# A delta-rule attention feeding two expert layers: the host transposes Q, and a block of Q is scaled by one number and split in place

## The chip, the cores and the metric

One core of a Trainium2 chip runs the whole program. The metric is device time in microseconds (us) of one execution, lower is better. Engines are named as in the profile: PE (matrix multiplies), PEld (its weight loads), DVE (vector), ACT (scalar/activation), POOL (GpSimd), SP (the queue that issues most transfers).

## The reference, cut to what matters

```
def _attn_ref(q, k, v, beta):                 # B=4, H=8, S=768, D=48
    k_n = k / (norm(k, axis=-1) + 1e-6)
    state = zeros((B, H, D, D))
    for t in range(S):
        y[:, :, t] = einsum('bhd,bhde->bhe', q[:, :, t], state)
        v_old = einsum('bhde,bhd->bhe', state, k_n[:, :, t])
        state = state + beta_t * einsum('bhd,bhe->bhde', k_n[:, :, t], v[:, :, t] - v_old)
    return y
# x = y as (3072, 384)
# x = moe(x):  8 experts, all of them on every row, weights from a Sinkhorn iteration on x @ w_gate
# out = moe2(x): 8 experts, one for each row (argmax), relu(x @ w1[e]) @ w2[e]
```

## The kernel before

Attention is cut into 12 chunks of 64 tokens; a chunk of two of the four batches is one **block**, so there are 24 blocks, `block(i)`. In a tile of a block, 128 partitions hold two batches by 64 tokens, or two batches by 64 places of which 48 are features, and the free axis holds the 8 heads. Numbers that need more than half precision are carried as two float16 tiles, a high part and a low part ("split"), and multiplied as three products.

For each block the **front** loads K, Q (one tile `KQ`, one transfer of `kq[c, pr]`) and V, takes sums of squares (`sqk`, `sqq`, `sqv` on ACT, the first ones reduced by `ssr` on DVE), normalises K (`rc1` to `rc5`, `kn`) and gets power-of-two scales (`scl`). K is split by `kh`, `kl`. Q has a scale for each of its rows: `qs` scales it, `qh` and `ql` split it into `KQ1[:, 2:4]`. K and Q each then go the same way: `kpd`/`qpd` put the two halves of the partitions into a block-diagonal tile (`KPB`, `QTB`) by two transfers on SP (for the first three blocks by copies on DVE and ACT), `kt0`, `kt1`/`qt0`, `qt1` (line 643) transpose on PE against an identity, 8 multiplies of 64 columns each, and `ke0`, `ke1`/`qe0`, `qe1` (lines 506 and 508, `kqc<-pz`) move the result from PSUM to the compact tile `KQc`, which has three buffers and has K in columns 0 to 63 of each head and Q in 64 to 127. From there `kb` and `qtd` make the block-diagonal `KTB` and `QTB` by further transfers, and `gp0`, `gp1` (line 660) multiply K by both. The rest of the block is a doubling recursion of five levels (`z`, `Z`, `a`, `t`, `tt`), the update of the state and the output (`y0`, `y1`, last score multiply `pl`, `lgs` on line 819).

At the same time `moe_unit` runs the first two experts on finished blocks: first-layer multiplies on line 849 (256 columns), second layer on 873 (384 columns), with ACT on 860 and 883 and DVE on 862. There are 2160 of these multiplies in 24 units. This overlapped stage is called the **weave** below. When its last unit is done, PE goes on with line 1085 and then with the other experts.

The order of all instructions of the weave on each engine is fixed when the program is built, by the class `Sched`: a list scheduler with a cost in ns for each operation, a priority (the block number less an advance) and free choice of engine where a node names several, as `(("A", 413), ("V", 270))`. So a changed cost or a changed node reorders the rest. Names of a node's engines: P is PE, A ACT, V DVE, G POOL, D the SP queue.

The next load into `KQ` waits for the last reader of the block before, since `KQ` has one buffer:

```
N("ld", "D", 1300, f, [("kl", pb), ("ql", pb), ("kn", pb), P4("r2l"), P4("sqv")] ...)
```

Of the kernel before, what the change touches and what calls it, by code (L numbers as in the profile page):

```python
# [19 lines left out]
C = 64  # L20
# [146 lines left out]
def kernel(  # L167
# [274 lines left out]
    with (  # L442
# [74 lines left out]
        def block(i):  # L517
# [21 lines left out]
            def front(name, shape, dt, at):  # L539
                if i == 1:  # L540
                    o[name] = hhl[:, at:at + (1 if dt is F16 else 2) * shape[0] * shape[1] * (shape[2] if len(shape) > 2 else 1)]
                    o[name] = o[name].bitcast(dt)
                    if len(shape) == 3:
                        o[name] = o[name].rearrange("p (a b c) -> p a b c", a=shape[0], b=shape[1])
                    else:
                        o[name] = o[name].rearrange("p (a b) -> p a b", a=shape[0])
                    return o[name]
                return tl(name, shape, dt, 0)
# [26 lines left out]
            def f():  # L575
                front("KQ1", [4, 8, 48], F16, 1536)
                tl("ss", [10], F32, par)
                nc.scalar.activation(out=o["KQ1"][:, 2], in_=o["Q"], func=AF.Square, accum_out=o["ss"][:, 8:9])
            N("sqq", "A", 510, f, ["ld", ("kpd", pb), ("qpd", pb), ("rc2", i - 2), ("par", i - 2)])
            N("sqv", "A", 510, lambda: nc.scalar.activation(  # L580
                out=o["KQ1"][:, 3], in_=o["V"], func=AF.Square, accum_out=o["ss"][:, 9:10]), ["sqq"])
# [4 lines left out]
            N("sq", "A", 220, lambda: nc.scalar.activation(out=tl("sr", [10], F32, par)[:, 0:9], in_=o["ss"][:, 0:9], func=AF.Sqrt),  # L586
              ["ssc", ("pq", i - 2), ("rc3", i - 2)])


            def f(slot):  # L590
                o["sv"] = pcp.tile([128, 1], F32, name="sv", tag=f"pc{slot}")
                nc.tensor.matmul(out=o["sv"], lhsT=ones32, rhs=o["ss"][:, 9:10], start=True, stop=True)
            N("sv", "P", 250, f, ["ssc"], ps=("pc", 1))
            N("par", "A", 200, lambda: nc.scalar.activation(out=o["sr"][:, 9:10], in_=o["sv"], func=AF.Sqrt), ["sv", "sq"], frees="sv")
            N("rc1", "V", 120, lambda: nc.vector.reciprocal(out=tl("rc", [8], F32, par), in_=o["sr"][:, 0:8]), ["sq", ("kn", i - 2)])
# [5 lines left out]
            N("kn", (("V", 470), ("G", 790)), 0, lambda e: ttt(e, o["K"], o["K"], o["rc"].unsqueeze(2).to_broadcast([128, 8, 48]), ALU.mult), ["rc5"])  # L601
            N("kh", (("A", 413), ("V", 270)), 0, lambda e: cpy(e, o["KQ1"][:, 0], o["K"]), ["kn"])
            N("kl", VG4, 0, lambda e: ttt(e, o["KQ1"][:, 1], o["K"], o["KQ1"][:, 0], ALU.subtract), ["kh"])

            BD("kpd", lambda: KPB[nb], lambda: o["KQ1"][:, 0:2], ["kl", P4("ds"), ("zK", nb)])

# [9 lines left out]
            else:  # L616
                NN[("pm", i)] = NN[("pq", i)]
            N("px_", "V", 70, lambda: nc.vector.tensor_scalar(
                out=o["scl"][:, 2:4].bitcast(U32), in0=o["scl"][:, 0:2].bitcast(U32), scalar1=EXPMASK, scalar2=None, op0=ALU.bitwise_xor), ["pm"])
            N("qs", "A", 507, lambda: nc.scalar.activation(out=o["Q"], in_=o["Q"], func=AF.Copy, scale=o["scl"][:, 2:3]), ["px_", "sqq"])  # L620
            N("vs", "A", 507, lambda: nc.scalar.activation(out=o["V"], in_=o["V"], func=AF.Copy, scale=o["scl"][:, 3:4]), ["px_", "sqv"])
            N("qh", (("A", 413), ("V", 270)), 0, lambda e: cpy(e, o["KQ1"][:, 2], o["Q"]), ["qs"])
            N("p3", "V", 75, lambda: nc.vector.tensor_tensor(
                out=o["scl"][:, 5:6], in0=o["scl"][:, 1:2], in1=c3[:, 1:2], op=ALU.mult), ["pm", ("cs", 0)])
            N("p4", "V", 70, lambda: stt(o["scl"][:, 7:8], o["scl"][:, 0:1], 0.125, o["scl"][:, 1:2], ALU.mult), ["pm"])
            N("ql", VG4, 0, lambda e: ttt(e, o["KQ1"][:, 3], o["Q"], o["KQ1"][:, 2], ALU.subtract), ["qh", "sqv"])

            BD("qpd", lambda: QTB[nb], lambda: o["KQ1"][:, 2:4], ["ql", P4("y1"), P4("qtd"), ("zQ", nb)])

# [5 lines left out]
            N("mb", (("V", 602), ("G", 1001)), 0, f, [("ml", i - NPS), ("m16", i - NPS), ("tt0", i - NPS), "kn", ("cs", 0), ("bt2", 0)])  # L635
            for x, nm, dep in ((0, "k", "kpd"), (1, "q", "qpd")):
                src = KPB[nb] if x == 0 else QTB[nb]
                for y in range(2):
                    def f(slot, x=x, y=y, src=src):
                        o["KQc"] = KQC[sl]  # L640
                        t = o[f"t{x}{y}"] = pzt(slot)
                        for h in range(H):
                            nc.tensor.matmul(out=t[:, h], lhsT=src[:, y, h], rhs=I16, start=True, stop=True)
                    N(f"{nm}t{y}", "P", 235, f, [dep, ("gp1", i - NPS), ("qtd", i - NPS), ("cs", 0)], ps=("pz", 1), cols=512)
                    N(f"{nm}e{y}", AV5, 0, lambda e, x=x, y=y: cpy(e, o["KQc"][:, y, :, 64 * x:64 * x + 64], o[f"t{x}{y}"]),
                      [f"{nm}t{y}"], frees=f"{nm}t{y}")
            BD("kb", lambda: KTB[nb], lambda: o["KQc"][:, :, :, 0:64], ["ke0", "ke1", P4("ks"), P4("gp1"), ("zT", nb)])

            def f():
                for b2 in range(2):  # L650
                    bd_half(QTB[nb], o["KQc"][:, :, :, 64:128], b2, nc.sync.dma_start)
            N("qtd", "D", 1300, f, ["qe0", "qe1"])
            for u in range(2):
                hs = slice(4 * u, 4 * u + 4)

                def f(slot, u=u):
                    pg = o[f"pg{u}"] = pzp.tile([128, 4, 128], F32, name="pg", tag=f"pz{slot}")
                    for h in range(4 * u, 4 * u + 4):
# [167 lines left out]
        def moe_unit(e, r):  # L826
# [14 lines left out]
            for g4 in range(nf // per):  # L841
                for j in range(per):
                    f_ = per * g4 + j
                    for kk in range(KD):
# [940 lines left out]
```

## Time and profile before

| | |
|---|---|
| median of 3 runs | 2178.95 us (2176.89 to 2179.65) |
| the profiled execution's own time | 2180.95 us |
| its span, first to last instruction | 2179.2 us |
| mean granted PE clock | 0.98 of full |
| busy: PE, DVE, ACT, POOL | 2052.1, 1230.6, 851.4, 261.5 us |

Busy times are shares of the whole span. The weave is its first 675 us; what an engine does there is read from that stretch alone. [...]

### The profile page before, as it was taken

What the parts mean: (1) busy time and instruction counts of PE and PEld (TensorE: products, weight loads), DVE (VectorE), ACT (ScalarE), POOL (GpSimd) and SP (SyncE); (2) the same over time, 40 slices, a digit from 0 to 9 for tenths busy, and PEclk for the clock granted to TensorE, in tenths of its full rate; (3) what the DMA queues carried; (4) which work ended last, traced back from release to release, by engine and by line L of the source; (5) the groups of instructions that cost most, each with busy time, mean ns of one, the idle gap of its engine ahead of it and who ended that gap; (6) DMA issues with size and microseconds to landing.
All of it is one profiled execution on the core that took longest, in us unless ns stands there. A gap on an engine that the chain in (4) does not pass through costs nothing. (4 is left out here: it accounts for less than half of the span.)

```text
span 2179.2 us, 46134 instructions
## 1 busy us (share of the span) xinstructions
PE 2052.1 (94%) x19340; PEld 1298.1 (60%) x19340; DVE 1230.6 (56%) x2828; ACT 851.4 (39%) x1598; POOL 261.5 (12%) x304
## 2 busy tenths in 40 slices
PE   4689999999998889999999999999999999999999
PEld 3567777777764435555555555555555555557776
DVE  7989888888771564555555455555552245552111
ACT  7766666666531332222222222222231134453332
POOL 3233232322200000000000000000000000113221
PEclk9699999999999989999999999999999999999999
DMA  7456655566534233113203113212300001058765
GB/s 255 91 110 116 120 108 111 114 122 129 124 90 167 95 99 116 55 62 116 88 30 116 59 58 117 87 44 102 116 30 1 1 15 30 19 174 331 257 236 205
DMA packets 372006, 235.14 MB, mean 108 GB/s; under 512 B 302588, under 2 KB 349600, under 8 KB 365394
## 3 DMA queue, kind: packets, MB, share of 16 engines
q1 hardware_dynamic: 366354, 220.32, 35.2%
q0 software_dynamic: 4288, 10.25, 1.4%
q8 instruction: 154, 2.52, 0.5%
q10 hardware_dynamic: 1152, 1.57, 0.2%
q14 instruction: 58, 0.48, 0.1%
HBM read 146.94 MB, written 51.93 MB: 91 GB/s over the span
## 5 line engine op out<-in xcount | busy, mean ns | idle before, releaser
L355 PE MATMUL pt<-big,W 128*128 128x512 f16 x2304 | 508.9, 381 | 9.3 <-DVE hhl L339 5.3
L355 PEld LDWEIGHTS <-W 128*128 128x128 f16 x2304 | 226.3, 98 | 281.4 <-issue 16.4
L366 PE MATMUL py<-W,hhl 128*128 128x384 f16 x1632 | 287.1, 327 | 3.5 <-DVE accb L385 3.4
L366 PE MATMUL py<-W,ttb 128*128 128x384 f16 x1440 | 253.6, 326 | 0.0
L338 ACT ACTIVATE hhl<-pt 128x512 f16<-128x512 f32 x136 | 81.1, 597 | 415.5 <-PE pt L355 415.3
L366 PEld LDWEIGHTS <-hhl 128*128 128x128 f16 x1632 | 160.1, 98 | 114.4 <-issue 6.0
L366 PEld LDWEIGHTS <-ttb 128*128 128x128 f16 x1440 | 140.9, 98 | 93.1
L385 DVE SCALAR_TENSOR_TENSOR accb<-py,pet,accb 128x384 f32<-128x384 f32 x136 | 83.8, 616 | 185.8 <-PE py L366 184.2
L849 PE MATMUL pt<-xring,W 128*128 128x256 f16 x1296 | 181.3, 278 | 2.2 <-ACT xring L506 1.0
L339 DVE SCALAR_TENSOR_TENSOR hhl<-pt,hhl 128x512 f16<-128x512 f32 x136 | 93.9, 690 | 153.1 <-ACT hhl L338 153.1
L873 PE MATMUL py<-W,hhl 128*128 128x384 f16 x864 | 175.3, 330 | 4.0 <-ACT yo L883 3.1
L339 DVE SCALAR_TENSOR_TENSOR ttb<-pt,ttb 128x512 f16<-128x512 f32 x120 | 83.0, 691 | 108.4 <-ACT ttb L338 108.4
L338 ACT ACTIVATE ttb<-pt 128x512 f16<-128x512 f32 x120 | 71.6, 597 | 151.4 <-PE pt L355 151.4
L298 DVE TENSOR_REDUCE wmx<-st 128x1 f32<-128x512 f32 x168 | 109.8, 676 | 33.2 <-DMA st<-in_moe_w_dram 33.2
L849 PEld LDWEIGHTS <-W 128*128 128x128 f16 x1296 | 115.4, 100 | 17.2 <-issue 1.8
L305 POOL PARTITION_ALL_REDUCE wma<-wm x28 | 10.1, 362 | 949.8 <-DVE wm L303 949.8
L1299 PEld LDWEIGHTS <-W 128*128 128x128 f16 x1008 | 90.7, 98 | 50.8 <-issue 0.3
L1319 PE MATMUL py<-W,hhl 128*128 128x384 f16 x624 | 108.9, 326 | 0.0
L1305 DVE SCALAR_TENSOR_TENSOR ttb<-pt,ttb 128x512 f16<-128x512 f32 x50 | 34.6, 692 | 117.7 <-ACT ttb L1304 117.7
L873 PEld LDWEIGHTS <-hhl 128*128 128x128 f16 x864 | 74.2, 100 | 41.5 <-issue 6.7
L1299 PE MATMUL pt<-big,W 128*128 128x512 f16 x432 | 97.7, 379 | 0.0
L1305 DVE SCALAR_TENSOR_TENSOR hhl<-pt,hhl 128x512 f16<-128x512 f32 x52 | 35.8, 688 | 87.2 <-ACT hhl L1304 87.1
(367 smaller groups left out, 3173.6 us busy)
## 6 DMA issues: line engine op xcount, KB each, us to landing
st<-in_moe_w_dram SPq DMA_DIRECT2D x28, 1536.0 KB, 9.5
W<-w2d SPq DMA_DIRECT2D x18, 1536.0 KB, 8.4
w2d<-big SPq DMA_DIRECT2D x16, 1536.0 KB, 6.2
big<-w2d SPq DMA_DIRECT2D x8, 1536.0 KB, 6.5
accb<-w2d SPq DMA_DIRECT2D x8, 1536.0 KB, 8.6
big<-kqc SPq DMA_DIRECT2D x90, 128.0 KB, 3.4
KQ<-in_kq_dram SPq DMA_DIRECT2D x23, 384.0 KB, 3.6
big<-KQ SPq DMA_DIRECT2D x84, 96.0 KB, 3.0
```

Of the source, the lines that this page charges most:

```text
L298: nc.vector.tensor_reduce(out=mx[:, c:c + 1], in_=st[:, c * CW:c * CW + CW], op=ALU.max, axis=AX.X, apply_absolute_value=True)
L305: nc.gpsimd.partition_all_reduce(ma, m1, channels=128, reduce_op=bass.bass_isa.ReduceOp.max)
L338: nc.scalar.activation(out=oh, in_=pt, func=AF.Relu)
L339: nc.vector.scalar_tensor_tensor(out=ol, in0=pt, scalar=0.0, in1=oh, op0=ALU.max, op1=ALU.subtract)
L355: nc.tensor.matmul(out=po, lhsT=lhsT, rhs=rhs, start=(i == 0), stop=(i == 3 * KD - 1))
L366: nc.tensor.matmul(out=py[:, 0:DM], lhsT=lhsT, rhs=rhs, start=(n == 0), stop=(n == 3 * (KF - fs) - 1))
L385: nc.vector.scalar_tensor_tensor(out=acc[t], in0=py[:, 0:DM], scalar=pe[x][:, t:t + 1], in1=acc[t], op0=ALU.mult, op1=ALU.add)
L849: nc.tensor.matmul(out=o[g4][:, 256 * j:256 * j + 256], lhsT=w1v(W, wv, kk, f_), rhs=XR[:, xv, kk], start=(kk == 0 and x == 0), stop=(kk = ...
L873: nc.tensor.matmul(out=o["py"][:, 0:DM], lhsT=a_[f_ // per][:, c_:c_ + 128], rhs=w2v(W, b_, f_), start=(f_ == 0 and x == 0), stop=(f_ == n ...
L1299: nc.tensor.matmul(out=po, lhsT=w1v(W, wv, kk, f), rhs=xv[:, kk, :], start=(kk == 0 and x == 0), stop=(kk == KD - 1 and x == 2))
L1305: V((f"rs{q_}", id_), lambda q_=q_: nc.vector.scalar_tensor_tensor(out=HL[q_], in0=o[q_], scalar=0.0, in1=HH[q_], op0=ALU.max, op1=ALU.sub ...
L1319: nc.tensor.matmul(out=o["py"][:, 0:DM], lhsT=a_[f // per][:, c_:c_ + 128], rhs=w2v(W, b_, f), start=(f == 0 and x == 0), stop=(f == KF - ...
```

## The change

The host writes Q as (feature, head, token) with 48 features padded to 64 places by zeros, so a row of `kq` grows from 768 to 896 numbers and Q comes in already transposed. `qh` on ACT multiplies Q by a scale and writes the high part straight into `KQc`; `ql` on DVE takes Q times the scale less that high part into the low half. `qs`, `qpd`, `qt0`, `qt1`, `qe0` and `qe1` are gone. Since rows of the new Q tile are features, the scale is one for the block: `sqq` squares 512 numbers in a row with 1/16 of each, and the multiply by ones that summed V's squares over partitions (`sv`) now sums a second column for Q.

```
 def f():
-    t = front("KQ", [2, 8, 48], F32, 0)
-    o["K"], o["Q"] = t[:, 0], t[:, 1]
-    nc.sync.dma_start(out=t.rearrange("p a h d -> p (a h d)"), in_=kq[c, pr])
+    t = front("KQ", [896], F32, 0)
+    o["K"], o["Q"] = t[:, 0:DM].rearrange("p (h d) -> p h d", h=8), t[:, DM:896].rearrange("p (h s) -> p h s", h=8)
+    nc.sync.dma_start(out=t, in_=kq[c, pr])
...
-    nc.scalar.activation(out=o["KQ1"][:, 2], in_=o["Q"], func=AF.Square, accum_out=o["ss"][:, 8:9])
-N("sqq", "A", 510, f, ["ld", ("kpd", pb), ("qpd", pb), ("rc2", i - 2), ("par", i - 2)])
+    nc.scalar.activation(
+        out=o["jk"][:, 0:512].rearrange("p (h s) -> p h s", h=8), in_=o["Q"], func=AF.Square, scale=1.0 / 16, accum_out=o["ss"][:, 8:9])
+N("sqq", "A", 620, f, ["ld", ("kpd", pb), ("rc2", i - 2), ("par", i - 2)])
...
-N("qs", "A", 507, lambda: nc.scalar.activation(out=o["Q"], in_=o["Q"], func=AF.Copy, scale=o["scl"][:, 2:3]), ["px_", "sqq"])
-N("qh", (("A", 413), ("V", 270)), 0, lambda e: cpy(e, o["KQ1"][:, 2], o["Q"]), ["qs"])
+o["KQc"] = KQC[sl]
+N("qh", "A", 620, lambda: nc.scalar.activation(
+    out=o["KQc"][:, 0, :, 64:128], in_=o["Q"], func=AF.Copy, scale=o["scl"][:, 2:3]), ["px_", "sqq", ("gp1", i - NPS), ("qtd", i - NPS)])
...
-N("ql", VG4, 0, lambda e: ttt(e, o["KQ1"][:, 3], o["Q"], o["KQ1"][:, 2], ALU.subtract), ["qh", "sqv"])
-
-BD("qpd", lambda: QTB[nb], lambda: o["KQ1"][:, 2:4], ["ql", P4("y1"), P4("qtd"), ("zQ", nb)])
+N("ql", "V", 602, lambda: stt(o["KQc"][:, 1, :, 64:128], o["Q"], o["scl"][:, 2:3], o["KQc"][:, 0, :, 64:128], ALU.subtract), ["qh"])
...
-N("qtd", "D", 1300, f, ["qe0", "qe1"])
+N("qtd", "D", 1300, f, ["ql", P4("y1"), P4("qtd"), ("zQ", nb)])
...
-N(f"gp{u}", "P", 680, f, ["kb", "qe0", "qe1"], ps=("pz", 2), cols=1536)
+N(f"gp{u}", "P", 680, f, ["kb", "ql"], ps=("pz", 2), cols=1536)
```

Line numbers behind the change move by two or three (643 becomes 641, 660 becomes 657, 849 becomes 846, 860 becomes 857, 873 becomes 870, 883 becomes 880, 1085 becomes 1082).

On ACT, in the front of a block in the middle of the weave, before: `qs` (620), the float16 copy of Q, V's scale (621) and evictions of transposes (`kqc<-pz`).

```order
L620 ACTIVATE KQ<-KQ,scl 128x384
L506 CAST KQ_5894<-KQ 128x384
L621 ACTIVATE V<-V,scl 128x384
L506 CAST kqc<-pz 128x8x64 x2
L883 COPY yo<-py 128x384
L506 CAST t_6148<-pz 128x512
L506 CAST tt<-pz 128x512
```

And at the same place of a block now:

```order
L620 ACTIVATE V<-V,scl 128x384
L506 CAST Et<-pz 128x512
L624 ACTIVATE kqc<-KQ,scl 128x8x64
L857 ACTIVATE hhl<-pt 128x512
L506 CAST R_6431<-V 128x384
L506 CAST t_6438<-pz 128x512
L506 CAST kqc<-pz 128x8x64 x2
```

Two passes over Q became one that writes `KQc` (line 624), and of four evictions for a block two are left. Over the whole weave ACT has 46 of them now and had 87; on DVE 2 are left of 9.

On DVE, in the same part of a block, before: the copy and the subtraction that split Q (both write `KQ_5894`, the tile `KQ1` of that block), between rows of the recursion and of `gp0`.

```order
L508 CAST KQ_5894<-KQ 128x384
L502 TENSOR_TENSOR Z<-pz,cs 128x512
L502 TENSOR_TENSOR KQ_5894<-KQ,KQ_5894 128x384
L690 STREAM_TRANSPOSE tt<-t_6148 128x512
L502 TENSOR_TENSOR W_99<-pg,W_99 128x256
L502 TENSOR_TENSOR PT<-pg,cs 128x256
```

And now, with the new subtraction `kqc<-KQ,scl,kqc`:

```order
L502 TENSOR_TENSOR Z<-pz,cs 128x512
L859 SCALAR_TENSOR_TENSOR hhl<-pt,hhl 128x512
L502 TENSOR_TENSOR W_99<-pg,W_99 128x256
L499 SCALAR_TENSOR_TENSOR kqc<-KQ,scl,kqc 128x8x64
L502 TENSOR_TENSOR PT<-pg,cs 128x256
L687 STREAM_TRANSPOSE tt<-t_5780 128x512
```

All 24 subtractions for Q stand on DVE now. In the whole weave DVE has 8 copies that split K or Q where it had 16, 15 such subtractions where it had 26, and 10 subtractions of the identity (`pi`, `W<-W,cs`) where it had 20: the other ten stand on POOL.

On ACT at the end of the attention, from the last block's copy into `xring` on, before:

```order
L506 COPY xring<-px 128x6x128
L860 ACTIVATE hhl<-pt 128x512
L984 ACT_TABLE_LOAD
L984 ACTIVATE P_103<-P_103 128x24x8
L956 ACTIVATE W_99<-st,w1s 128x512 x3
L883 COPY yo<-py 128x384 x2
L860 ACTIVATE hhl<-pt 128x512 x2
L883 COPY yo<-py 128x384 x2
L860 ACTIVATE hhl<-pt 128x512 x4
```

And now:

```order
L506 COPY xring<-px 128x6x128
L857 ACTIVATE hhl<-pt 128x512 x2
L981 ACT_TABLE_LOAD
L981 ACTIVATE P_103<-P_103 128x24x8
L880 COPY yo<-py 128x384
L953 ACTIVATE W_99<-st,w1s 128x512 x3
L880 COPY yo<-py 128x384
L857 ACTIVATE hhl<-pt 128x512 x4
L880 COPY yo<-py 128x384 x2
```

Behind the last block stand 16 hidden-layer passes (860, now 857) where 11 stood, so more of the expert units' work lies behind the attention. On PE the last score multiply stands behind 1692 of the 2160 expert multiplies; it stood behind 1812. Of the 120 that moved behind it 96 are of the first layer (849) and 24 of the second (873).

## Rows read from the trace of the kernel before

**Rows 1.** The page's head, and PE's granted clock in 40 slices of the span.
```profile
span 2179.2 us, 46134 instructions
...
PEclk9699999999999989999999999999999999999999
```

**Rows 2.** Windows: stretch, length, busy time and count of each engine, clock, DMA share.
```profile
20.00:60.00 40.00, 19.67 (x307) 17.39 (x308) 38.55 (x109) 30.96 (x63) 16.04 (x15) 0.99 0.73 205
60.00:100.00 40.00, 26.57 (x525) 23.52 (x525) 38.66 (x93) 29.54 (x56) 10.22 (x10) 0.63 0.35 69
100.00:600.00 500.00, 462.82 (x8843) 373.90 (x8840) 423.13 (x995) 311.18 (x664) 136.89 (x126) 0.97 0.59 118
600.00:675.00 75.00, 69.05 (x635) 49.69 (x631) 44.95 (x131) 23.54 (x41) 2.25 (x7) 0.98 0.26 79
```

**Rows 3.** Groups of instructions to 660 us: busy us, mean ns, idle before.
```profile
L506 ACT CAST kqc<-pz 128x512 f16<-128x512 f32 x87 | 48.7, 585 | 9.4 <-PE pz L643 8.9
...
L643 PE MATMUL pz<-c,big 128*128 128x64 f16 x768 | 38.2, 202 | 14.7 <-ACT kqc L506 4.4 <-DVE Z L502 4.4 <-ACT big L506 4.3
...
L502 POOL TENSOR_TENSOR KQ<-KQ,KQ 128x384 f16<-128x384 f32 x21 | 20.3, 969 | 25.2 <-ACT KQ L506 13.7 <-DVE KQ L508 9.4 <-ACT V L621 1.8
...
L502 DVE TENSOR_TENSOR KQ<-KQ,KQ 128x384 f16<-128x384 f32 x25 | 16.8, 674 | 1.9 <-ACT KQ L506 1.6
...
L506 ACT CAST KQ<-KQ 128x384 f16<-128x384 f32 x31 | 15.7, 505 | 4.4 <-POOL KQ L502 3.8 <-DVE KQ L502 0.4
...
L620 ACT ACTIVATE KQ<-KQ,scl 128x384 f32<-128x384 f32 x23 | 14.2, 617 | 19.8 <-DVE scl L618 19.5
...
L572 ACT ACTIVATE K<-KQ 128x384 f32<-128x384 f32 x23 | 12.1, 524 | 23.6 <-DMA KQ<-in_kq_dram 22.7 <-DVE ss L582 0.7
...
L578 ACT ACTIVATE KQ<-KQ 128x384 f16<-128x384 f32 x23 | 11.8, 513 | 3.0 <-DMA KQ<-in_kq_dram 3.0
...
L508 DVE CAST KQ<-KQ 128x384 f16<-128x384 f32 x15 | 8.6, 572 | 1.2 <-ACT KQ L620 1.2
...
L508 DVE CAST kqc<-pz 128x512 f16<-128x512 f32 x9 | 6.1, 680 | 0.0
```

**Rows 4.** Two adjacent rows of PE's timeline: start, length, line, count.
```profile
558.08 0.63 PE L643 MATMUL pz<-c,big 128*128 128x64 f16 x16
558.55 0.65 PE L873 MATMUL py<-W,hhl 128*128 128x384 f16 x3
```

**Rows 5.** The same view of groups: nearest kin of the new instructions, and `pi`.
```profile
L502 DVE TENSOR_TENSOR W<-W,cs 128x512 f32<-128x512 f32 x20 | 14.2, 712 | 0.0
...
L958 DVE SCALAR_TENSOR_TENSOR W<-xring,w0s,W 128x512 f16<-128x512 f32 x9 | 7.8, 873 | 1.1 <-ACT W L956 1.1
...
L956 ACT ACTIVATE W<-xring,w0s 128x512 f16<-128x512 f32 x9 | 6.0, 715 | 0.0
...
L502 POOL TENSOR_TENSOR W<-W,cs 128x512 f32<-128x512 f32 x4 | 5.1, 1271 | 13.3 <-DVE W L502 13.3
...
L958 DVE SCALAR_TENSOR_TENSOR W<-st,w1s,W 128x512 f16<-128x512 f32 x3 | 2.2, 739 | 0.0
```

**Rows 6.** Timeline of the weave's end: last block's result, expert multiplies, next stage.
```profile
617.31 0.23 DVE L819 TENSOR_SCALAR lg<-pl,scl 128x8 f32<-128x8 f32 x1
...
653.11 4.06 PE L873 MATMUL py<-W,hhl 128*128 128x384 f16 x24 [0.61 <-ACT yo L883]
...
657.00 4.09 PE L849 MATMUL pt<-xring,W 128*128 128x256 f16 x36
...
660.93 2.40 PE L873 MATMUL py<-W,hhl 128*128 128x384 f16 x12
...
674.78 7.93 PE L1085 MATMUL pt<-big,W 128*128 128x512 f16 x36
```

**Rows 7.** Transfers to 675 us: count, KB of each, median us from issue to landing.
```profile
KQ<-in_kq_dram SPq DMA_DIRECT2D x23, 384.0 KB, 3.6
big<-KQ SPq DMA_DIRECT2D x84, 96.0 KB, 3.0
```

More of the change, by code (lines that the diff above doesn't have):

```diff
@@ L540, in front @@
                 if i == 1:
-                    o[name] = hhl[:, at:at + (1 if dt is F16 else 2) * shape[0] * shape[1] * (shape[2] if len(shape) > 2 else 1)]
-                    o[name] = o[name].bitcast(dt)
+                    n_ = shape[0] * (shape[1] * shape[2] if len(shape) > 1 else 1)
+                    o[name] = hhl[:, at:at + (1 if dt is F16 else 2) * n_].bitcast(dt)
                     if len(shape) == 3:
                         o[name] = o[name].rearrange("p (a b c) -> p a b c", a=shape[0], b=shape[1])
-                    else:
-                        o[name] = o[name].rearrange("p (a b) -> p a b", a=shape[0])
                     return o[name]
@@ L575, in f @@
             def f():
-                front("KQ1", [4, 8, 48], F16, 1536)
+                front("K1", [2, 8, 48], F16, 1792)
                 tl("ss", [10], F32, par)
-                nc.scalar.activation(out=o["KQ1"][:, 2], in_=o["Q"], func=AF.Square, accum_out=o["ss"][:, 8:9])
-            N("sqq", "A", 510, f, ["ld", ("kpd", pb), ("qpd", pb), ("rc2", i - 2), ("par", i - 2)])
+                o["jk"] = o["K1"].rearrange("p a h d -> p (a h d)")
+                nc.scalar.activation(
+                    out=o["jk"][:, 0:512].rearrange("p (h s) -> p h s", h=8), in_=o["Q"], func=AF.Square, scale=1.0 / 16, accum_out=o["ss"][:, 8:9])
+            N("sqq", "A", 620, f, ["ld", ("kpd", pb), ("rc2", i - 2), ("par", i - 2)])
             N("sqv", "A", 510, lambda: nc.scalar.activation(
-                out=o["KQ1"][:, 3], in_=o["V"], func=AF.Square, accum_out=o["ss"][:, 9:10]), ["sqq"])
+                out=o["jk"][:, 0:DM].rearrange("p (h d) -> p h d", h=8), in_=o["V"], func=AF.Square, accum_out=o["ss"][:, 9:10]), ["sqq"])
             N("ssr", "V", 480, lambda: nc.vector.tensor_reduce(
@@ L585, in block @@
                 out=o["ss"], in0=o["ss"], scalar1=2.0 ** -18, scalar2=1e-30, op0=ALU.mult, op1=ALU.max), ["ssr", "sqv"])
-            N("sq", "A", 220, lambda: nc.scalar.activation(out=tl("sr", [10], F32, par)[:, 0:9], in_=o["ss"][:, 0:9], func=AF.Sqrt),
+            N("sq", "A", 220, lambda: nc.scalar.activation(out=tl("sr", [10], F32, par)[:, 0:8], in_=o["ss"][:, 0:8], func=AF.Sqrt),
               ["ssc", ("pq", i - 2), ("rc3", i - 2)])
             def f(slot):
-                o["sv"] = pcp.tile([128, 1], F32, name="sv", tag=f"pc{slot}")
-                nc.tensor.matmul(out=o["sv"], lhsT=ones32, rhs=o["ss"][:, 9:10], start=True, stop=True)
+                o["sv"] = pcp.tile([128, 2], F32, name="sv", tag=f"pc{slot}")
+                nc.tensor.matmul(out=o["sv"], lhsT=ones32, rhs=o["ss"][:, 8:10], start=True, stop=True)
             N("sv", "P", 250, f, ["ssc"], ps=("pc", 1))
-            N("par", "A", 200, lambda: nc.scalar.activation(out=o["sr"][:, 9:10], in_=o["sv"], func=AF.Sqrt), ["sv", "sq"], frees="sv")
+            N("par", "A", 200, lambda: nc.scalar.activation(out=o["sr"][:, 8:10], in_=o["sv"], func=AF.Sqrt), ["sv", "sq"], frees="sv")
             N("rc1", "V", 120, lambda: nc.vector.reciprocal(out=tl("rc", [8], F32, par), in_=o["sr"][:, 0:8]), ["sq", ("kn", i - 2)])
@@ L601, in block @@
             N("kn", (("V", 470), ("G", 790)), 0, lambda e: ttt(e, o["K"], o["K"], o["rc"].unsqueeze(2).to_broadcast([128, 8, 48]), ALU.mult), ["rc5"])
-            N("kh", (("A", 413), ("V", 270)), 0, lambda e: cpy(e, o["KQ1"][:, 0], o["K"]), ["kn"])
-            N("kl", VG4, 0, lambda e: ttt(e, o["KQ1"][:, 1], o["K"], o["KQ1"][:, 0], ALU.subtract), ["kh"])
-            BD("kpd", lambda: KPB[nb], lambda: o["KQ1"][:, 0:2], ["kl", P4("ds"), ("zK", nb)])
+            N("kh", (("A", 413), ("V", 270)), 0, lambda e: cpy(e, o["K1"][:, 0], o["K"]), ["kn"])
+            N("kl", VG4, 0, lambda e: ttt(e, o["K1"][:, 1], o["K"], o["K1"][:, 0], ALU.subtract), ["kh"])
+            BD("kpd", lambda: KPB[nb], lambda: o["K1"], ["kl", P4("ds"), ("zK", nb)])
             def f():
@@ L635, in block, with f @@
             N("mb", (("V", 602), ("G", 1001)), 0, f, [("ml", i - NPS), ("m16", i - NPS), ("tt0", i - NPS), "kn", ("cs", 0), ("bt2", 0)])
[L636 to L646, printed above, removed]
+            for y in range(2):
+                def f(slot, y=y):
+                    t = o[f"t{y}"] = pzt(slot)
+                    for h in range(H):
+                        nc.tensor.matmul(out=t[:, h], lhsT=KPB[nb][:, y, h], rhs=I16, start=True, stop=True)
+                N(f"kt{y}", "P", 235, f, ["kpd", ("gp1", i - NPS), ("qtd", i - NPS), ("cs", 0)], ps=("pz", 1), cols=512)
+                N(f"ke{y}", AV5, 0, lambda e, y=y: cpy(e, o["KQc"][:, y, :, 0:64], o[f"t{y}"]), [f"kt{y}"], frees=f"kt{y}")
             BD("kb", lambda: KTB[nb], lambda: o["KQc"][:, :, :, 0:64], ["ke0", "ke1", P4("ks"), P4("gp1"), ("zT", nb)])
@@ L856, in moe_unit @@
                             dep.append(("mlast", last))
-                            dep += [("kpd", 1), ("qpd", 1), ("kn", 1), ("qs", 1)]
+                            dep += [("kpd", 1), ("kn", 1), ("qh", 1), ("ql", 1)]
                         N(nm, "P", 327, f, dep, ps=("pt", 1) if j == 0 and kk == 0 else None, cols=768, moe=True)
@@ L1764, in add @@
         args.append(nc.dram_tensor(f"in_{name}_dram", a.shape, _mybir.dt.from_np(a.dtype), kind="ExternalInput").ap())
-    q_, k_, v_ = (_np.reshape(inputs[n], (2, 2, H, NC, C, D)).transpose(3, 0, 1, 4, 2, 5).reshape(NC, 2, 128, H * D) for n in "qkv")
-    inputs["kq"] = _np.concatenate([k_, q_], -1)
+    k_, v_ = (_np.reshape(inputs[n], (2, 2, H, NC, C, D)).transpose(3, 0, 1, 4, 2, 5).reshape(NC, 2, 128, H * D) for n in "kv")
+    qt_ = _np.zeros((NC, 2, 2, C, H, C), _np.float32)
+    qt_[:, :, :, 0:D] = _np.reshape(inputs["q"], (2, 2, H, NC, C, D)).transpose(3, 0, 1, 5, 2, 4)
+    inputs["kq"] = _np.concatenate([k_, qt_.reshape(NC, 2, 128, H * C)], -1)
     inputs["v"] = v_
```

## The prediction

> **What bounds the kernel now.** I read the page's head and slices first: the span is 2179.2 us and PE's clock is full nearly throughout, with one dip in the second slice [rows 1]. The windows cut the span where its nature changes [rows 2]. From 20 to 100 us DVE is busy 77.2 of 80 us while PE is about half busy: DVE sets the pace of the ramp. From 100 to 600 us PE is busy 463 of 500 us (93%), DVE 423 (85%), ACT 311 (62%), POOL 137 (27%). So in the long part of the weave PE is nearest to full and DVE second. From 600 to 675 us PE is busy 69 of 75. The timeline of the end shows the border: the last block's result comes at 617.3, then PE works off what is left of the expert units, and the next stage's first multiply starts at 674.8 [rows 6]. From there to the end of the span are 2179.2 - 674.8 = 1504.4 us whose code and order the change leaves alone. So the change can only move the point 674.8, by what it does to PE's work or to PE's waits.
>
> **PE.** Gone are `qt0` and `qt1`: 24 blocks x 2 x 8 = 384 of the 768 multiplies on line 643 (with their weight loads). The mean record of 202 ns [rows 3] is not their price, since records overlap. Sixteen of them start at 558.08 and the next line starts at 558.55 [rows 4], so 0.47/16 = 29.4 ns each, and 384 x 29.4 ns = **11.3 us**. This is at the full clock; in the ramp some run at half of it, but there PE is not what is waited for.
>
> [...]
>
> **ACT.** Gone: 24 `qs` at 617 ns and 41 evictions at 585 ns, 14.8 + 24.0 us; copies that split K or Q fall from 32 to 15, 17 x 505 ns = 8.6 us [rows 3]. New: 24 `qh` over 512 numbers with a scale read per partition, nearest kin line 956 at 715 ns [rows 5], +17.2 us; and `sqq` over 512 numbers where 384 took 513 ns [rows 3], by the step from 617 to 715 ns for the same growth +0.1 us x 24 = +2.4. Net about -28 us on an engine 62% busy: no gain by itself, but fewer late evictions.
>
> **DVE.** Gone of Q's and K's splitting: 8 copies (16 to 8) x 572 ns, 11 subtractions (26 to 15) x 674 ns, 7 evictions x 680 ns: 4.6 + 7.4 + 4.8 = 16.8 us [rows 3]. New: 24 `ql` in one pass over 512 numbers; kin line 958 took 739 ns undisturbed and 873 ns beside the weight loading of the ramp [rows 5], so 17.7 to 21.0 us. I take 17.7, since the ramp holds only the first few of 24 blocks. So the Q work on DVE comes out even (+0.9, at worst +4.2). It had been shared with POOL, which loses 13 of its 21 subtractions. What DVE does gain is that ten `pi` move to POOL: -10 x 712 ns = -7.1 us, against +10 x 1271 ns on POOL, which stood idle three quarters of the time [rows 2, 5]. Net about -6 us, bounds -7 to -3.
>
> **SP and transfers.** 42 of the 84 transfers of 96 KB from `KQ1` go, and each load grows from 384 to 448 KB [rows 7]. That removes 4.0 MB and adds 1.5 MB. DMA is 59% busy in the weave [rows 2]; I put the gain at nothing (bounds 0 and -2 us), because the waits ahead of line 643 name ACT and DVE [rows 3]. Q's path to `gp0` loses a transfer of 3.0 us, the transposes and the evictions, but K still goes that way, so `gp0` comes no sooner on that account.
>
> **Where the work goes.** The built order moves 120 expert multiplies behind the last block. From the end of the weave, 24 of the second layer take 657.00 - 653.11 = 3.89 us (162 ns) and 36 of the first 660.93 - 657.00 = 3.93 us (109 ns) [rows 6], so these 120 are 96 x 0.109 + 24 x 0.162 = 14.4 us. If PE sets the pace, the attention ends 11.3 + 14.4 = 25.7 us sooner, near 592, and the tail grows from 57.5 to 71.9 us: a gain of 11.3 at the end. If DVE sets it, the gain is its 6 us, and what PE saves turns into PE idle time. PE at 93% is nearer to full than DVE at 85%, so I stay near PE's end but not on it: **-9 us** (bounds -5 and -14). Against the profiled execution's own 2180.95 us that is 2172; this execution lay 2.0 us above the median 2178.95, so the median becomes **2170**.
>
> A difference of 0.2%, 4.4 us, is about what a measurement of this kernel can tell from none.
>
> **Rivals.**
> *More goes than the work.* Line 643 waited 14.7 us in all for evictions and PSUM buffers, and the evictions 8.9 us for it [rows 3]; half of these transposes and 48 of 96 evictions are gone. If Q's half of the waits goes (7.4 us) and ACT's relief removes a few more, the gain is 16 to 25 us: 2154 to 2163. For it: the three PSUM buffers `pz` are asked for 48 times less. Against it: PE follows a fixed order, and a wait removed at one row is often met again at the next.
>
> *DVE takes it all.* `ql` can no longer be given to POOL, and behind it on DVE stand the recursion's `Z` and `tt`, for which PE waits. If 24 x 873 ns is the price and the ten `pi` on POOL (1271 for 712 ns, ahead of `tt0` and `m16`) hand their extra 0.56 us on, the gain is 6 - 3.2 - 5.6 = -2.8, so within 4 us of none: 2175 to 2182. For it: DVE at 97% in the ramp. Against: 15% of its time free after that.
>
> *Slower: the load waits.* `KQ` has one buffer, and `ql` now cannot run before a buffer of `KQc` is free, so the next block's load starts when `ql` is done and takes 3.6 us to land [rows 7]. ACT already waits 22.7 us for these loads [rows 3], and in the new order fewer instructions stand on ACT between `qh` and the next block's first square. ACT is in order: behind that square wait the evictions for PE. If each of 23 loads costs PE 1 us more, the time is 2170 + 23 = 2193; it is slower from 13.4/23 = 0.6 us a block on. Against it: the same load waited for `ql` before too, behind `qs` and `qh`, and ACT is idle 38% of the time.
>
> [...]
>
> **How the numbers follow.** Forecast (5 to 14 us less): 0.53. More than the work: 0.18. DVE takes it: 0.17. The load waits: 0.08. The clock: 0.04. Faster by over 0.2%: the first two, less a little at the forecast's edge, 0.70; within 0.2%: 0.18, the third and that edge; slower: the last two, 0.12. The range 2158 to 2181 holds the forecast, the third case but for its edge and half of the second; what lies outside is about 0.2. The forecast's own range is 2165 to 2174.
>
> **What would show it.** In the profile after: 384 multiplies on line 641; `qh` at 0.70 to 0.73 us on ACT and `ql` at 0.72 to 0.88 us on DVE; the last `lg` between 590 and 605 us and the first multiply of line 1082 between 660 and 670; from there to the end 1504 us within 3. PE's busy time from 100 to 600 stays at 93% or above. I am wrong in the size if PE's busy share falls while DVE's rises above 90%; wrong in the sign if ACT's wait for `KQ<-in_kq_dram` grows to 45 us or more and PE's idle time grows with it, or if the clock stays near 0.6 behind 100 us. If the attention ends early but line 1082 starts at 675, the tail has eaten the gain.

## The result, and the profile after

The change made the kernel slower: 2192.6 us median (2186.5 to 2197.8, 7 runs) against 2178.8 us for the kernel before on the same chip, a ratio of 1.0057, 95% interval [1.0046, 1.0069]. (Ratios are given as they stand on record; the quotient of two medians, here 1.0063, differs from them by up to 0.1%.) I had forecast 2170 and a range of 2158 to 2181. The profiled execution after has a span of 2191.2 us.

The page's head and clock after, to be read against [rows 1]:

```profile
span 2191.2 us, 45238 instructions
...
PEclk9999999999999999999999999999999999999999
```

The windows after, with the columns of [rows 2]:

```profile
20.00:60.00 40.00, 17.32 (x238) 14.85 (x239) 31.50 (x89) 27.61 (x57) 11.59 (x11) 1.00 0.66 217
60.00:100.00 40.00, 22.14 (x400) 19.93 (x400) 38.99 (x91) 22.86 (x44) 12.37 (x11) 1.00 0.43 82
100.00:600.00 500.00, 451.36 (x8593) 361.73 (x8593) 417.33 (x992) 303.10 (x631) 142.58 (x129) 0.96 0.54 113
600.00:675.00 75.00, 70.83 (x620) 51.34 (x619) 44.13 (x124) 23.31 (x40) 2.26 (x7) 1.00 0.21 66
```

From 100 to 600 us PE is busy 11.5 us less than before, DVE 5.8 and ACT 8.1 less. All three engines do less, and all three stand idle longer; PE's share is 90%, where the prediction wanted 93% or above. Part of this is work that now stands behind 600 us. Over the whole weave, in which both kernels do the same expert work, PE is busy 577.5 us (583.4 before), DVE 545.7 (555.2) and ACT 388.1 (406.5). The windows give a clock of 1.00 from 60 to 100 us, where before it was 0.63, but twelve multiplies of line 657 take 1.44 to 1.46 us there (at 62.8, 89.3 and 91.8 us), as long as at 0.50 and not 0.84 as at 1.00 (rows in the last section).

The end of the weave after, to be read against [rows 6] (DVE's and PE's timelines):

```profile
616.54 0.23 DVE L816 TENSOR_SCALAR lg<-pl,scl 128x8 f32<-128x8 f32 x1 [2.10 <-PE pl L813]
```
```profile
687.10 7.93 PE L1082 MATMUL pt<-big,W 128*128 128x512 f16 x36
```

This is the whole loss. The last scores come at 616.5 us where they came at 617.3, and not near 592 as forecast. The 120 expert multiplies that the new order puts behind them make the tail 70.6 us long where it was 57.5: +13.1, forecast +14.4. From 687.1 to the end are 1504.1 us, before 1504.4. The attention got 0.8 us shorter, the tail 13.1 longer, and the span 12.0. The orders in the table further below bear the tail's part out: in the changed kernel it takes 38.9 us with 246 multiplies behind the last scores and 77.9 us with 516, 0.14 us more for each.

The groups of the new and the halved Q path to 660 us, to be read against [rows 3] and [rows 5]:

```profile
L506 ACT CAST kqc<-pz 128x512 f16<-128x512 f32 x46 | 25.7, 586 | 3.9 <-PE pz L641 3.9
L499 DVE SCALAR_TENSOR_TENSOR kqc<-KQ,scl,kqc 128x512 f16<-128x512 f32 x23 | 21.0, 915 | 3.1 <-ACT kqc L624 3.0
L641 PE MATMUL pz<-c,big 128*128 128x64 f16 x384 | 20.0, 204 | 8.4 <-DVE big L508 3.5 <-ACT big L506 3.5 <-DVE Z L502 0.6
...
L624 ACT ACTIVATE kqc<-KQ,scl 128x512 f16<-128x512 f32 x23 | 16.3, 711 | 0.0
L577 ACT ACTIVATE K<-KQ 128x512 f16<-128x512 f32 x23 | 14.3, 620 | 5.8 <-DMA KQ<-in_kq_dram 5.8
```

`qh` took 711 ns where I had 715, `sqq` 620 where I had 615, the wait ahead of the transposes fell from 14.7 to 8.4 us. `ql` took 915 ns on average where I had taken 739. The longest waits of PE from 100 to 600 us (total, times, longest) are now these:

```profile
PE pz L483 <- DVE Z L502: 9.8, 13, 1.7
PE pc L483 <- ACT Et L506: 4.9, 4, 2.1
PE sv L592 <- DVE ss L584: 4.2, 2, 3.9
PE pz L694 <- DMA W<-t: 2.9, 4, 1.6
```

No single one is large: PE stands a little longer at many places.

### The profile page after: what moved, and what is told of

The parts are those of the page before. It is cut to its first block, busy times and chain, and to the rows that moved or that the text cites. A ratio compares the mean times of both kernels' runs of the same rounds, so it can differ in the third digit from the quotient of the medians.

```text
span 2191.2 us, 45238 instructions
## 1 busy us (share of the span) xinstructions
PE 2043.9 (93%) x18956; PEld 1288.2 (59%) x18956; DVE 1221.2 (56%) x2804; ACT 833.0 (38%) x1544; POOL 265.4 (12%) x304
```

## The experiments

In all kernels the share of PE time that the planner gives to the expert units is the constant `SH0`, 0.50 in both kernels. It is a handle on the order: a changed share gives the same work in another order. "Order" takes in the choice of engine, where a node names several: of the 24 `pi`, POOL has 4 in the kernel before, 14 in the changed kernel and 12 in the changed kernel at 0.48. "Last scores" is the last block's `lg`, "ahead" the number of the 2160 expert multiplies that stand before the last score multiply `pl`. Each ratio is against the kernel before, run beside it on the same chip.

### First: is it the work or the order?

**e3_old_order.** The work of the changed kernel in the order of the kernel before. The planner still gets the old nodes; those that are gone issue nothing, and `qh` and `ql` are issued where the old evictions of Q stood. To make that free of hazards `KQ` has two buffers, and to make room for them the small tile `wg_s` lies inside `hhl`.

```
+N("qs", "A", 507, lambda: None, ["px_", "sqq"])
+N("qh", (("A", 413), ("V", 270)), 0, lambda e: None, ["qs"])
...
+N(f"{nm}e{y}", AV5, 0, lambda e, x=x, y=y: qsplit() if x else cpy(...), [f"{nm}t{y}"], frees=f"{nm}t{y}")
```

> The changed work in the order of before: the scheduler still sees the removed nodes with their old costs, but they issue nothing; the new scaling of Q on ACT is issued where the first eviction of Q stood, the new subtraction on DVE where the second stood. KQ has two buffers here so that the old order stays legal. 1812 expert multiplies stand before the last block's scores, as before. Theory A (the new order is at fault: the attention has its own pace, and 120 expert multiplies were pushed behind it): the attention ends at 617 us or up to 10 us sooner, the weave 658 to 674 us, time 2165 to 2178. Theory B (the new instructions themselves cost: the 0.9 us subtraction on DVE and the late reload of K and Q): the weave ends at 680 us or later, time 2185 to 2195 in either order.

Measured: 2181.6 us, ratio 1.0005 [0.9988, 1.0021], between the two theories' ranges; the last scores and the weave's end:

```profile
619.52 0.23 DVE L830 TENSOR_SCALAR lg<-pl,scl 128x8 f32<-128x8 f32 x1
```
```profile
675.85 7.93 PE L1096 MATMUL pt<-big,W 128*128 128x512 f16 x36
```

The removed work, in the old order, brought nothing that can be measured, though ACT was busy 22 us less in the weave (384.5 and 406.5). The loss of 12 us does not come with the work in this order; it came with the new order. Two limits: the `pi` stay where the old plan has them (20 on DVE), so DVE is not relieved here (busy 556.3 us, 555.2 before). And the second buffer is part of this kernel; alone it moved the time by -0.27% to +0.35% in three other orders (g1, g2, g3 below), so it could hide up to 8 us of gain. The kernel before with two buffers was not run.

**e1_share55, e4_share70, e2_before_share60.** Other shares: the changed kernel with 0.55 and 0.70, the kernel before with 0.60.

```
-SH0 = 0.5
+SH0 = 0.55
```

> The changed kernel with one constant changed, the share of PE that the scheduler grants the expert units, SH0 from 0.50 to 0.55: 1914 instead of 1692 of 2160 expert multiplies stand before the last block's scores. Theory A (PE has idle time inside the attention that expert multiplies can fill): the attention ends at 617 to 627 us, the tail falls from 70.6 to 40 to 45 us, the weave ends at 657 to 672, time 2162 to 2177. Theory B (the weave is short of PE or DVE time anyway): the attention ends 222 multiplies later, at 640 us or more, and the weave again near 685 to 690, time 2190 within 5.

Measured: 2178.8 us, 0.9988 [0.9976, 1.0000]; 1914 ahead, last scores at 635, weave's end 674.8. The last scores and the time lie between the two theories. More expert work ahead of the last scores takes the loss back, without a gain.

> The changed kernel with SH0 0.70: 1950 expert multiplies before the last block's scores, and more of them early in the weave. Theory A: within 4 us of the run with 0.55, the attention ending a few us later and the tail a few us shorter. Theory B: slower than the changed kernel, over 2195.

Measured: 2249.3 us, 1.0315 [1.0287, 1.0342]; 1950 ahead, last scores at 705. That leaves Theory A out, and is 54 us past Theory B's bound.

> The kernel before with SH0 0.60, which puts 1920 expert multiplies before the last block's scores, to set beside the changed kernel with 1914. If the share alone makes the difference, this one gains as much as the changed kernel does from it, and the changed kernel at the same share is 5 to 12 us faster than this one by its 11 us of PE work. If the old kernel has no room left on PE (93% busy), it stays within 4 us of 2179 and the changed one at best equals it.

Measured: 2217.5 us, 1.0173 [1.0141, 1.0205]; 1920 ahead, last scores at 671. Neither expectation held. The count alone does not decide: in the kernel before 1920 ahead gave 671 here and 635 at share 0.54, and in the changed kernel 1914 ahead gave a ratio of 0.9988 at 0.55 and of 0.9935 at 0.54 (table below).

### Second: what sets the attention's pace?

**e7_two_products.** The changed kernel in its own order, with two of the three products of each expert multiply of the weave.

```
-for x, (wv, xv) in enumerate(((0, 0), (0, 1), (1, 0))):
+for x, (wv, xv) in enumerate(((0, 0), (0, 1))):
```

> The changed kernel in its own order, but of the three products of each expert multiply of the weave only two are made (720 of 2160 multiplies left out, 564 of them before the last scores; the outputs of those experts lose their smallest part). At 109 and 162 ns a multiply that takes some 74 us of PE's work from before the attention's end. If PE sets the attention's pace, the last scores come near 543 us instead of 616. If the attention's own chain of dependent steps on DVE, ACT and PE sets it, they stay above 600, PE's busy share from 100 to 600 us falls to about 75%, and only the tail behind the attention gets shorter, by a third of its 70 us.

Measured: 2173.6 us, 0.9972 [0.9959, 0.9984]. The window, and the end of the attention and of the weave:

```profile
100.00:600.00 500.00, 411.36 (x8136) 324.44 (x8133) 421.24 (x1005) 305.06 (x637) 142.43 (x130) 0.93 0.55 114
```
```profile
610.34 0.23 DVE L816 TENSOR_SCALAR lg<-pl,scl 128x8 f32<-128x8 f32 x1 [1.71 <-PE pl L813]
```
```profile
669.35 7.93 PE L1082 MATMUL pt<-big,W 128*128 128x512 f16 x36
```

Some 74 us of PE's work ahead of the last scores are gone by the prediction's prices from start to start (PE's busy time up to 610 us fell by 41 us), and the last scores come 6.2 us sooner. The mean granted clock of the window was 0.93 where it was 0.96. In the trace of the changed kernel it is 0.50 from 422 to 428 us, and six multiplies of line 870 there take 1.89 us to the next row's start (423.72 to 425.61), 0.315 us each, where one costs 0.162 at 1.00. By these numbers the lower level held for an estimated 30 us longer, which took back an estimated 15 us of the 74. PE's work alone does not set the attention's pace in this order. Behind the attention it counts, though not in full: the tail fell from 70.6 to 59.0 us, 11.6 us, where a third of its 468 multiplies are 17 to 25 us at 109 to 162 ns.

**e8_no_low.** The changed kernel in its own order without DVE's 72 passes on line 859. The third product then counts the high half a second time.

```
-N(f"rs{g4}", "V", 602, lambda g4=g4: nc.vector.scalar_tensor_tensor(out=hl[g4], ...
+N(f"rs{g4}", "V", 602, lambda: None, [(f"rl{g4}", u)],
...
-for x, (a_, b_) in enumerate(((hh, 0), (hh, 1), (hl, 0))):
+for x, (a_, b_) in enumerate(((hh, 0), (hh, 1), (hh, 0))):
```

> The changed kernel in its own order without the 72 passes on DVE that make the low half of the experts' hidden layer (678 ns each, 56 of them before the last scores: 38 us of DVE's 417); the third product reads the high half instead, so PE's work is the same and the experts' output is less exact. If DVE's work sets the attention's pace, the last scores come 30 us or more sooner, below 590. If the length of the chain or PE's order sets it, they come within 10 us of 616.

Measured: the weave's end at 679.9, the last scores here:

```profile
100.00:600.00 500.00, 452.51 (x8687) 364.50 (x8687) 394.93 (x954) 306.17 (x639) 143.34 (x130) 0.97 0.55 114
```
```profile
610.42 0.23 DVE L816 TENSOR_SCALAR lg<-pl,scl 128x8 f32<-128x8 f32 x1 [2.10 <-PE pl L813]
```

DVE is busy 22 us less in this window and 27 us less up to 610 us (509.0 and 482.1; by my sum 38), and the last scores come 6.1 us sooner. DVE's work alone does not set the pace either. The whole time, 2199.9 us (1.0103 [1.0081, 1.0124]), is not comparable: the experts' output is another one, so routing behind the weave works on other numbers, and from the weave's end on this kernel took 1517 us instead of 1504.

**h1_share48_two_products, h2_before_two_products.** The same cut of a third in a fast order of the changed kernel (0.48, below) and in the order of the kernel before.

> The changed kernel at share 0.48 (last scores at 593 us) with two of the three products of each expert multiply of the weave: 548 of the 1644 multiplies before the last scores are left out, about 72 us of PE. If every order has its own floor from its waits and the one at 0.50 merely has a high one (610 us), the last scores come well before 593, at 575 or sooner. If waits set the pace in every order and PE's work in none, they stay between 583 and 593.

Measured: 2147.3 us, 0.9862 [0.9841, 0.9882].

```profile
589.81 0.23 DVE L816 TENSOR_SCALAR lg<-pl,scl 128x8 f32<-128x8 f32 x1 [1.08 <-PE pl L813]
```

> The kernel before in its own order with two of the three products of each expert multiply: 604 of 1812 multiplies before the last scores left out, about 79 us of PE. The old order did not come sooner by the 11 us of transposes. If its waits set the pace, the last scores stay above 605 (617 with all the work). If PE sets it, they come near 540, and the missing gain of the transposes needs another reason.

Measured: 2164.3 us, 0.9943 [0.9925, 0.9961].

```profile
615.46 0.22 DVE L819 TENSOR_SCALAR lg<-pl,scl 128x8 f32<-128x8 f32 x1
```

3.1 us sooner than 592.9 with all the work, and 1.9 us sooner than 617.3 [rows 6]. In three orders of two kernels the last scores stay where the order puts them, though 72 to 79 us of PE were taken away by the same prices (41 to 53 us of its busy time). By the same token 11.3 us of transposes could hardly show.

### Third: how far does the order alone move the time?

**Eight orders.** Shares 0.48, 0.52 and 0.54 for both kernels; the edit is the constant.

> The changed kernel with the planner's share at 0.48: 1644 expert multiplies before the last scores, 48 fewer than at 0.50. If the attention keeps its own pace, its last scores come near 610 to 617 us again and the tail grows by some 6 us: 2190 to 2200. If the particular order decides by several us, the time can lie anywhere from 2175 to 2205.

> The changed kernel at 0.52: 1854 expert multiplies before the last scores. If the count decides, the time lies between that at 0.50 (2193 us, 1692) and that at 0.54 (2164 us, 1914): 2168 to 2176. If the attention keeps its own pace up to some count, its last scores come at 615 to 625 us.

> The changed kernel with the planner's share of PE time for the experts at 0.54 instead of 0.50; nothing else differs. As many expert multiplies stand before the last scores as with 0.55 (1914), in another order. If the time depends on the particular order and not on the work, this order may differ from the one at 0.55 (0.9988 of before) by several us in either direction although both do the same work. If instead the number of expert multiplies before the last scores decides, it gives 0.997 to 1.000, as 0.55 did.

> The kernel before at 0.48: 1698 expert multiplies before the last scores, nearly the count of the changed kernel at 0.50. If the count decides, this kernel loses what the changed one lost by it: the last scores near 612 to 617 us, the tail 14 us longer than at 0.50, and 2188 to 2194 in all. If the changed kernel lost its 13 us for another reason, this one stays within 5 us of 2179.

> The kernel before at 0.52: 1830 expert multiplies before the last scores, 18 more than at 0.50. By the count 2177 to 2182. By the order alone anywhere from 2172 to 2192.

> The kernel before with the same 0.54. If the kernel before at 0.50 is a lucky order among its neighbours, and the changed work is really cheaper from order to order, this is slower than before (1.003 or more) and slower than the changed kernel at 0.54. If the orders of before are all alike, it is within 0.2% of before.

Measured (ratio and interval; ahead; last scores; weave's end, us):

| share | changed kernel | kernel before |
|---|---|---|
| 0.48 | 0.9937 [0.9920, 0.9955]; 1644; 592.9; 670.8 | 1.0045 [1.0027, 1.0062]; 1698; 606; 677.9 |
| 0.50 | 1.0057 [1.0046, 1.0069]; 1692; 616.5; 687.1 | 1; 1812; 617.3; 674.8 |
| 0.52 | 0.9985 [0.9968, 1.0003]; 1854; 621; 674.0 | 0.9953 [0.9938, 0.9968]; 1830; 624; 674.9 |
| 0.54 | 0.9935 [0.9915, 0.9955]; 1914; 628.6; 667.5 | 1.0027 [1.0014, 1.0040]; 1920; 635; 677.3 |

With the same work the time moves by 1.2% in the changed kernel and 0.9% in the kernel before. At 0.48 the changed kernel does what I forecast for 0.50, last scores at 592.9:

```profile
592.90 0.23 DVE L816 TENSOR_SCALAR lg<-pl,scl 128x8 f32<-128x8 f32 x1 [1.26 <-PE pl L813]
```
```profile
670.80 7.93 PE L1082 MATMUL pt<-big,W 128*128 128x512 f16 x36
```

At 0.50 it has 48 more multiplies ahead (at 109 to 162 ns, 5 to 8 us of PE), but the last scores come 23.6 us later: the order at 0.50 is the worst of the four. The lateness does not come at one place: the tenth block's scores come at 307.6 us at 0.50 and 309.3 at 0.48, the twelfth's at 354.9 and 343.4, the twentieth's at 538.2 and 518.6. Two of the six, the changed kernel at 0.48 (2164.3 us) and the kernel before at 0.52 (2168.9 us), were faster than anything I had expected of them: the order moves the time further than I had allowed. The mean over the four shares is 0.9979 for the changed kernel and 1.0006 for the one before, 0.28% or 6 us apart; the four differences (-0.0108, +0.0057, +0.0032, -0.0092) scatter by three times that, so four pairs do not show that the change is worth anything.

The table has one thing more. From its first to its last row the last scores come 0.13 us later for each multiply more ahead of them, in both kernels (592.9 to 628.6 over 270, 606 to 635 over 222), and the entries between lie within 4 us of these two lines, but for the changed kernel at 0.50, which lies 17 us above its line. At like counts the changed kernel's line is some 6 us below the other. 0.13 us is about what a multiply costs on PE (0.109 to 0.162 us from start to start), and about what it costs in the tail (0.14 us), so moving multiplies behind the attention is nearly even, as I had it in the sum; the order at 0.50 is the exception. This does not name PE as the bound: an expert unit that stands ahead brings its passes on ACT and DVE along. Nor is it a rule for all orders: the orders at 0.55, 0.60 and 0.70 lie 6, 35 and 72 us above these lines.

**g4_old_order52.** The old-order test again, in the order that the kernel before has at 0.52.

> The changed work in the exact order that the kernel before has at share 0.52 (2169 us with the old work). If removing the work gives nothing while the order stands, as it did in the order at 0.50, 2166 to 2172. If the missing gain there was particular to that order, up to 11 us less: 2157 to 2165.

Measured: 2166.0 us, 0.9937 [0.9918, 0.9957], beside 0.9953 [0.9938, 0.9968] with the old work in that order. The difference, -0.16%, lies within the two intervals: the removed work again brings nothing that can be measured, with the same two limits.

### Fourth: the load into one buffer

**g1_two_loads, g2_share48_two_loads, g3_share54_two_loads.** `KQ` gets two buffers (with `wg_s` inside `hhl`, as above), the order stays.

```
-return tl(name, shape, dt, 0)
+return tl(name, shape, dt, i % 2 if name == "KQ" else 0)
```

> The changed kernel in its own order at 0.50, but the tile of K and Q has two buffers, so the next block's load is issued at the same place and no longer waits for the last reader of the block before. If the load behind the new subtraction makes the attention late, ACT's wait for loads (18.8 us from 100 to 600 us) falls by more than half, the last scores come near 600 and the time falls to 2178 to 2184. If the order's other waits take its place, the time stays at 2188 to 2193.

Measured: 2196.3 us, 1.0079 [1.0054, 1.0103]; last scores at 617.3, weave's end 687.8. ACT's wait for loads from 100 to 600 us after, and with two buffers:

```profile
ACT K L570 <- DMA KQ<-in_kq_dram: 18.8, 10, 5.1
```
```profile
ACT K L570 <- DMA KQ<-in_kq_dram: 19.9, 10, 3.7
```

The wait did not go: the single buffer alone was not what made ACT wait. The load rival falls for this order.

> The same two buffers with the share at 0.48, the order that gave 2164 us. If loads cost time in every order, it gains 3 us or more: 2155 to 2161. If not, 2161 to 2167.

> The same two buffers with the share at 0.54, the other order that gave 2164 us; there ACT waits 24.7 us for loads from 100 to 600 us, more than in the slow order at 0.50. If loads cost time in every order, it gains most of the three: 2150 to 2158. If not, 2161 to 2167.

Measured: 2172.4 us, 0.9972 [0.9958, 0.9986], worse than 0.9937 with one buffer and than both expectations; and 2160.4 us, 0.9908 [0.9881, 0.9935], where one buffer gave 0.9935 [0.9915, 0.9955]. Opposite signs: the second buffer is no gain by itself. The last is the fastest version with all the reference's work, and faster than both kernels, though its interval overlaps with that of one buffer.

The chain that ended last passes through the weave in the trace of g1, whose order is that of the changed kernel. Its shares from 100 to 617 us:

```profile
by line: PE pt L846 11.4%; issue 11.4%; PE py L870 9.9%; PE pz L483 3.5%; PE pc L488 3.3%; PE pc L771 3.2%; DMA KQ<-in_kq_dram 3.2%; DVE Z L502 3.0%; DVE tt L687 2.2%; DMA big<-kqc 2.1%; PE pz L488 2.1%; DMA W<-t 1.8%; PE pg L657 1.6%; SPq 
1094 pieces in order of time: start us, us, what
```

517 us in 1094 pieces, 0.47 us each on average (the longest are 9.6 us of issue and 6.8 us of a load into `KQ`), over all engines and many lines, the two of the expert multiplies at the top with 21%. Yet a third of those multiplies gone gained 6 us, not a third of 21% of 517 us (37 us). That other chains lie close behind this one would explain it; no run shows it.

## Why the prediction was wrong

**The step that failed** is "If PE sets the pace, the attention ends 11.3 + 14.4 = 25.7 us sooner, near 592", with the ground given for it, "PE at 93% is nearer to full than DVE at 85%, so I stay near PE's end". The attention ended 0.8 us sooner. The runs show that busy shares named no pace: with 41 us (by records) to 74 us (by starts) less for PE (e7), or 27 to 38 us less for DVE (e8), it ended 6 us sooner, and h1 and h2 show the first in two more orders. In its place they show that the end of the attention goes with the planned order, from 593 to 629 us in four orders of the changed kernel: by how many multiplies the plan puts ahead, and by how it lays them, which at 0.50 cost 17 us against its neighbours' line. There the gain that moving 120 multiplies should have brought did not come, and the tail's price stayed. That the order acts through many short waits between engines that take their instructions in turn is read from the list of waits and the chain, and shown by no run of its own. The alternative "if DVE sets it, the gain is its 6 us" fails by e8. It was also wrong as a sum, for it left out the tail: if PE does not set the pace, the 120 multiplies still stand behind the attention, and 6 us of gain against 14.4 us of tail are a loss of 8 us.

**What was right.** That the change can move only the weave's end: 1504.1 us behind it. The tail's term: +13.1 measured, 14.4 forecast. That 384 transposes go; their price of 11.3 us was measured by no run, and PE's busy time in the weave, by records, fell by 5.9 us. That a multiply moved behind the attention should cost about what it saves there, by the lines through the other orders. The last sentence of the prediction, on a tail that eats the gain, came near to what happened, but there was no gain to eat.

**What was mis-sized.** `ql`: 23 of them took 21.0 us, which is the upper bound I gave for all 24, not 17.7. That bound's 873 ns, the mean of nine operations of line 958, is not shown to come from the weight loading: seven of the nine took 0.73 to 0.75 us, and the two others 1.53 (at 39.03 us) and 1.08 (at 104.74), each with a POOL operation begun 0.4 us before it. It did not decide: e3 and g4 contain the same `ql`. ACT: 28 us less forecast, 18.4 us less busy in the weave, without weight in the sum.

**The rivals.** "More than the work goes": the waits of line 641 did fall, by 6.3 us, and the attention ended no sooner for it, as its own counter-argument said. It had misread 4.3 of the 14.7 us, which were waits for ACT's copies into K's block-diagonal tile (`big`) and not for evictions or buffers; waits for `big` are most of the 8.4 us that are left. "The load waits": ACT's wait for loads from 100 to 617 us was 18.8 us where it was 21.1, and g1 took the buffer away as a reason. "The clock", to which I gave 0.04: PE was emptier in the ramp than before (17.3 of 40 us, then 22.1, where it had 19.7 and 26.6), and its multiplies ran slowly in more of it. Twelve of line 657 took 1.44 to 1.46 us at six places from 44.9 to 91.8 us, and 0.84 at 106.3; before, the same twelve took 0.84 at 55.1 and 57.3 and 1.44 to 1.46 at 48.7, 50.7, 80.4 and 83.0. From 100 to 600 us the mean clock was 0.96, before 0.97. What slow multiplies in the ramp cost in time is shown by no run; at share 0.54, a fast order (0.9935), twelve took 1.46 us at 56.1 too. No rival had the mechanism that came: an order that pays the 14.4 us of the tail and gets nothing for it in the attention.

**What stays open.** Which of the many waits makes the order at 0.50 late by 23.6 us against that at 0.48 is not found; only the load's buffer was excluded. PE and DVE lightened at once was not tried, nor ACT alone in the new order. Whether the change is worth something on the mean over orders needs more than four pairs: the 6 us between the two lines would speak for it, the two tests in the old order against it.

## What to carry to other kernels

Where a planner lays out every engine's instructions in a fixed order, a change to the work is also a draw of a new order, and here the draw moved the time by 1%, while the work's own worth (0.28% on the mean of four pairs) could not be told from nothing. Test the work in the old order and the new order apart, and try a few neighbouring settings of the planner before judging either kernel. Before counting on a busy engine, ask what the end does when a third of that engine's work is left out; one run answers it for that engine alone.

## What the runs showed of the hardware

`ql` takes 0.74 us alone and up to 1.65 us where a POOL operation had begun just before it. DVE's and POOL's timelines of the changed kernel at one such place:

```profile
358.45 1.65 DVE L499 SCALAR_TENSOR_TENSOR kqc<-KQ,scl,kqc 128x512 f16<-128x512 f32 x1
360.02 0.70 DVE L687 STREAM_TRANSPOSE tt<-t 128x512 f16<-128x512 f16 x1
```
```profile
358.28 1.27 POOL L502 TENSOR_TENSOR W<-W,cs 128x512 f32<-128x512 f32 x1 [0.38 <-DVE W L502]
```

POOL ends at 359.55 and `ql` at 360.10, 0.55 us later. Of 23 `ql`, 17 took 0.73 to 0.75 us, five 1.28 to 1.65 us and one 0.93 us. Each of these six had a POOL operation begun 0.1 to 0.5 us before it, and each ended 0.54 or 0.55 us after that operation. Why is shown by no run.

The granted clock that the windows give for the ramp differed between runs without a trace in the work. The first two windows at share 0.52 and then at 0.54:

```profile
20.00:60.00 40.00, 17.31 (x238) 14.85 (x239) 32.00 (x90) 27.63 (x58) 12.08 (x11) 0.51 0.64 215
60.00:100.00 40.00, 22.49 (x416) 20.05 (x415) 38.99 (x90) 22.76 (x43) 11.81 (x11) 0.59 0.43 83
```
```profile
20.00:60.00 40.00, 17.31 (x238) 14.84 (x239) 31.98 (x90) 27.48 (x57) 11.97 (x11) 1.00 0.65 215
60.00:100.00 40.00, 22.44 (x416) 20.20 (x415) 39.00 (x90) 22.71 (x43) 11.92 (x11) 1.00 0.43 82
```

Two rows of PE's timeline, at 0.52 and at 0.54:

```profile
55.98 1.46 PE L657 MATMUL pg<-kqc,big 128*128 128x128 f16 x12
```
```profile
56.10 1.46 PE L657 MATMUL pg<-kqc,big 128*128 128x128 f16 x12
```

With a granted clock of 0.51 or of 1.00, the same 238 multiplies were busy for the same 17.31 us, the same rows began within 0.12 us of each other up to here, and the sixth block's scores came at 214 and 217 us. The kernel before has the same twelve multiplies (there line 660) at these places; the windows over them give 1.00, 1.00, 0.50 and 1.00:

```profile
48.73 1.46 PE L660 MATMUL pg<-kqc,big 128*128 128x128 f16 x12
```
```profile
55.10 0.84 PE L660 MATMUL pg<-kqc,big 128*128 128x128 f16 x12
```
```profile
80.35 1.46 PE L660 MATMUL pg<-kqc,big 128*128 128x128 f16 x12
```
```profile
102.04 0.84 PE L660 MATMUL pg<-kqc,big 128*128 128x128 f16 x12
```

At 80.35 and 102.04 us the length goes with the clock; at 48.73 the twelve take as long under 1.00 as under 0.50, and so they do at share 0.54. In the ramp the column does not tell how fast the multiplies ran; their own rows do.
